# Cosine attention into a gated FFN on one core: 64-row products in five tiles, seven-product val one unit earlier, later loads of a batch, and a newly listed order

## The chip, the cores and the metric

The kernel runs on one core of a Trainium2 chip. The metric is device time in microseconds, the median over runs. A core has TensorE (PE; its weight loads are listed as PEld), VectorE (DVE), ScalarE (ACT), GpSimd (POOL) and SyncE (SP). Each engine runs its own list of instructions in order, and semaphores make one wait for another. DMAs are issued by SP, GpSimd and ScalarE. SBUF holds the data on 128 partitions; PSUM has eight banks of 128 x 512 fp32, into which TensorE writes.

## The reference

Eight batches, eight heads, 576 positions, 64 features a head. The attention is linear: the positive part of q and k is weighted by a cosine and a sine of the position, so that a head has 128 features, and

```python
r = np.maximum(x, 0.0)
phi(x) = np.concatenate([r * cos_w, r * sin_w], axis=-1)
kv = np.einsum('bhsf,bhsd->bhfd', phi(k), v)
z = np.sum(phi(k), axis=2)
num = np.einsum('bhsf,bhfd->bhsd', phi(q), kv)
den = np.einsum('bhsf,bhf->bhs', phi(q), z)[..., None] + 1e-06
attn = num / den
```

The result, as 4608 tokens of 512 features, goes through a gated feed-forward block with 1536 hidden features:

```python
g = x @ w_gate
val = x @ w_val
out = (g * sigmoid(g)) * val @ w_out
```

## The kernel before

**Tiles and groups.** A tile is 128 tokens: two slots of 64 positions of one batch, or the last slot of a batch and the first of the next (a two-batch tile: 4, 13, 22, 31). There are 36 tiles; four of them make a token group of 512 tokens, so there are nine groups, 0 to 8. For each batch the keys and values (`raw_kv`) become a key-value matrix per head, with z as a 65th column (`kv_job`, 72 products on quarters of the array). The queries become phi (`r_q`), which one DMA transpose turns (`phit`). For the first batches, tiles 4 to 8, TensorE turns the queries itself (`turned_tiles`), so that the cosine part and the sine part of a pair of heads lie in separate operands, which two accumulated products join. `tile_jobs` then computes a tile: products into two banks (L779 for tiles 4 to 8, L785 for the others), the denominator on ScalarE, its reciprocal and the multiplication on VectorE (`x`), and the turn of x (`turn_job`): by TensorE for tiles 4 to 7, by a DMA transpose on SP from tile 8 on. The DMA's turn is called a tile's turn below.

**The feed-forward block.** The 1536 hidden features are three units of 512 for gate and three for val. A plain product job is four products of 512 columns for 128 hidden features (`plain_fc`, `plain_val`, L904 and L1052), four of them a unit. The other form, `block_jobs`, computes a unit by the seven products of Strassen's scheme in Winograd's form, M1 to M7, each of four products with 256 columns (L977); sums of weights (`weight_sums`) and of x (`x_sum_jobs`) are made by VectorE. M1 is copied to a second bank (ScalarE), M7 is evacuated (`m7`), an addition puts M7 on M6 (VectorE), M5 is followed by a second addition, and M3 goes into the bank which that addition reads. `GATE_FROM` and `VAL_FROM` say from which group and unit on the seven products are used: gate from group 1, unit 0; val from group 2, unit 1. `silu_jobs` and `block_mul_jobs` form the hidden values `ht`; `token_sum_jobs` sums them; `out_jobs` makes the outputs with seven products P1 to P7 of the same kind (L1142). Group 0 is plain (`plain_out_jobs`, L1262).

**The order.** The first 27 us are a list written out by hand (`words`). All later work is a list of jobs. A planner (`order_once`) walks through modelled time with a cost for each job, due times, the banks and buffers that are free, and random shifts of the due times drawn by `SEEDS`, one seed for each `WINDOW` of modelled time; jobs are then issued in the order of their modelled starts. What it models decides only the order: on the chip, semaphores decide.

**Loads.** GpSimd issues the loads and most stores. The loads of a batch stand behind a hold, a tiny copy on GpSimd (`hold_job`) that reads what an earlier transfer wrote and so keeps the queue waiting for it. For batch 3 the hold reads the turn of tile 8; for the others it reads phi of the batch before, or for queries the turn of the last tile of a group.

Of the kernel before, what the change touches and what calls it, by code (L numbers as in the profile page):

```python
# [19 lines left out]
def kernel(  # L20
# [385 lines left out]

    xT = {}
# [175 lines left out]
    TAIL = {"PE": 206.0, "ACT": 160.0, "DVE": 140.0, "POOL": 150.0, "SP": 150.0}  # L583
    PAD = 12.0
# [19 lines left out]
    def sc(n, sbuf=False):  # L604
        return 69 + n / 1.2 + (27 if sbuf else 0) + PAD

# [29 lines left out]
    def relu_on(eng, out, in_):  # L636
# [11 lines left out]
    LOADED = {("k", 1): 440.0, ("v0", 1): 7580.0, ("v1", 1): 9080.0, ("sa", 1): 10080.0, ("sb", 1): 14480.0, ("q", 2): 22280.0,  # L648
              ("k", 2): 25580.0, ("v", 2): 29580.0, ("q", 3): 32380.0}
    WO_AT = ((0, 2, 11330.0), (2, 4, 12580.0), (4, 8, 16980.0), (8, 12, 19480.0))  # L650
    W_AT = {8: (1750.0, 3060.0), 10: (4820.0, 6130.0)}
# [19 lines left out]
    DEN_ON = {"ACT": 100}  # L671
# [35 lines left out]
    def kv_job(b, key, after):  # L707
# [12 lines left out]
        mm = pe(1404, fn, key, after=after, get=[r], chore=b > 1)  # L720
        outs = []
        for n in range(2):
            for i in range(2):
# [8 lines left out]
                outs.append(Job({"ACT": 402, "DVE": 450} if b == 1 else {"ACT": 402}, fn, after=[mm] + J_.get(("tiles", b - 2), []), put=[r]))  # L732
# [11 lines left out]
    def turn_job(t, x, after, by_pe=False, key=None):  # L744
        if not by_pe:
            def fn(j):
                nc.sync.dma_start_transpose(out=xT_of(t), in_=one(x_all, x))
            J_["xT", t] = Job({"SP": 1450}, fn, after=after + J_.get(("xT_read", t // OUT - 3), []), put=[x], tail=X_LAND, dma=(1430.0, X_SVC))
            return
        r = Room("bank")  # L750

        def fn(j):
            ps = bank(r).bitcast(FP16).rearrange("p (k x) -> p k x", x=P)
            for kc in range(KC):
                nc.tensor.transpose(out=ps[:, kc], in_=one(x_all, x)[:, kc * P:(kc + 1) * P], identity=ident16)
        mm = pe(230, fn, key, after=after, get=[r], put=[x])
# [5 lines left out]
    X_LAND = 4000.0  # L762
    X_SVC = 1030.0
    PHI_LAND = 11500.0

    def tile_jobs(t, key, by_pe=False):
# [3 lines left out]
        def fn(j):  # L770
            ps = bank(r)
            for e in range(2):
                for g in range(G):
                    for ms, b, c, n in parts_of(t):
                        if b < 2:
                            if g % 2:
                                continue
                            for w in range(2):
                                nc.tensor.matmul(  # L779
                                    out=ps[ms, e, g * D1:(g + 2) * D1],  # L780
                                    lhsT=late[:, 2 * (t % 2) + w, e, g // 2].rearrange("p c s -> p (c s)")[:, ms],
                                    rhs=(kvd1 if b else kvd)[:, e, g // 2, w].rearrange("p i x -> p (i x)"),
                                    start=w == 0, stop=w == 1)
# [5 lines left out]
        mm = pe(690 if 0 in bs else 455 if 1 in bs else 520 if len(bs) == 2 else 262, fn, key, after=sum((J_["kv", b] + turned_for(b, t) for b in bs), []), get=[r, one_at], chore=not by_pe)  # L789

        def view():
            return bank(r)[:, :, 0:2 * J * D1].rearrange("p e (y x) -> p e y x", x=D1)

        def fn(j):
            o, i_ = den_all[:, t % 4].rearrange("p (e y) o -> p e y o", e=2), view()[:, :, :, D:D1]
# [8 lines left out]
        rec = Job({"DVE": 132}, fn, after=[den])  # L804

        def fn(j):
            tt(out=one(x_all, x).rearrange("p (y e d) -> p e y d", e=2, d=D), in0=view()[:, :, :, 0:D],  # L807
               in1=rec_all[:, t % 4].rearrange("p (e y) o -> p e y o", e=2).to_broadcast([P, 2, 4, D]), op=ALU.mult)
# [8 lines left out]
    def load_job(b, nm, after, lands, behind):  # L817
        def fn(j):
            (load_turned if nm == "q" else load)(b, nm)
        J_["load", b, nm] = Job({"POOL": 1600 if nm == "q" else 780}, fn, after=after, tail=lands, behind=behind, dma=(1940.0, 2460.0) if nm == "q" else (470.0, 3770.0))  # L820

    def hold_job(read, after, put=()):
        def fn(j):
            nc.gpsimd.tensor_copy(out=hold2, in_=read())
        jb = Job({"POOL": 480}, fn, after=after, put=put)
# [854 lines left out]
```

## Time and profile before

| | |
|---|---|
| median of 3 runs | 298.38 us (298.32 to 298.6) |
| span of the profiled execution, first to last instruction | 296.4 us |
| TensorE busy | 291.1 us, 3244 products |
| VectorE busy | 252.0 us, 514 instructions |
| ScalarE busy | 199.4 us |
| GpSimd busy | 69.6 us |
| granted TensorE clock, mean | 0.998 |

The span is 2.0 us shorter than the median of the runs: what lies before its first and behind its last instruction isn't in it. Times in the profile's rows count from the span's start. A row of the chain gives the start, the duration and the group with its number of products; a row of the groups gives total busy time, mean ns of one, and the idle time ahead of it with what ended it. The end of a product is modelled: a group's shown end lies some 0.16 us behind the start of the next.

### The profile page before, as it was taken

To read this page: it belongs to the slowest core of one execution; us is meant where nothing else is said; L and a number is where in the kernel's file an instruction comes from. 1 tells how busy PE (TensorE), PEld (TensorE's weight loads), DVE (VectorE), ACT (ScalarE), POOL (GpSimd) and SP (SyncE) were. 2 spreads that over 40 slices of the span, in tenths; PEclk is the share of its full clock that TensorE was granted. 3 is DMA by queue.
4 is the path that set the end of the run, shared out by engine and by line. 5 is a ranking of instruction groups with operands and counts; after the bars stand their busy time and mean duration, and the time that the engine had idled before them with its cause. 6 is when DMAs were issued, how large, how long until landed. Compare 5 with 4: busy or idle time off the path is not lost.

```text
span 296.4 us, 8073 instructions
## 1 busy us (share of the span) xinstructions
PE 291.1 (98%) x3244; PEld 238.7 (81%) x3244; DVE 252.0 (85%) x514; ACT 199.4 (67%) x421; POOL 69.6 (23%) x122
## 2 busy tenths in 40 slices
PE   8999999999999999999999999999999999999994
PEld 4597465776787888898898889888988888888883
DVE  7878997879877999999988987998679868986883
ACT  6564346989559968985699589967465556565630
POOL 7963630003007012221352023200220050002000
PEclk9999999999999999999999999999999999999999
DMA  7999999997989997799996979940470046002026
GB/s 266 225 196 198 202 206 207 203 205 121 194 177 144 229 190 122 151 171 149 174 203 133 186 113 162 183 81 2 107 110 2 0 97 119 2 0 73 0 58 157
DMA packets 71973, 40.89 MB, mean 138 GB/s; under 512 B 48768, under 2 KB 68736, under 8 KB 71936
## 3 DMA queue, kind: packets, MB, share of 16 engines
q0 software_dynamic: 24800, 24.39, 49.1%
q1 hardware_dynamic: 46528, 15.47, 28.9%
q10 hardware_dynamic: 608, 0.52, 0.7%
q8 instruction: 25, 0.41, 0.6%
q14 instruction: 12, 0.10, 0.1%
HBM read 37.75 MB, written 9.44 MB: 159 GB/s over the span
## 4 chain that ended last, share of the span: by engine, by line
PE 97%; DVE 1%; issue 0%
PE banks L977 45%; PE banks L1142 24%; PE banks L1052 5%; PE banks L1262 4%; PE banks L438 4%; PE banks L904 4%; PE banks L187 3%; PE banks L716 3%; PE banks L785 2%; PE banks L779 1%; PE banks L372 1%; PE banks L1310 0%; PE banks L315 0%; PE banks L418 0%; PE banks L351 0%
## 5 line engine op out<-in xcount | busy, mean ns | idle before, releaser
L1111 POOL DMA_DIRECT2D out_dram<-ob x52 | 27.3, 532 | 104.8 <-ACT ob L630 69.7
L1036 ACT ACTIVATE sg<-banks 128x512 bf16<-128x512 f32 x72 | 41.3, 599 | 5.6 <-PE banks L977 5.4
L977 PEld LDWEIGHTS <-wg_sb 128*128 128x128 f16 x384 | 36.9, 98 | 6.3
L628 ACT COPY banks<-banks 128x512 f32<-128x512 f32 (+1 forms) x53 | 29.9, 572 | 17.5 <-PE banks L977 7.3
L1142 PEld LDWEIGHTS <-ht 128*128 128x128 f16 x384 | 37.4, 98 | 4.8
L1072 DVE TENSOR_TENSOR ht<-sg,banks 128x512 f16<-128x512 bf16 x60 | 39.9, 680 | 0.9 <-PE banks L977 0.6
L977 PEld LDWEIGHTS <-wgs_sb 128*128 128x128 f16 x368 | 35.7, 98 | 4.6
L997 DVE TENSOR_TENSOR banks<-m,banks 128x512 f32<-128x512 f32 x44 | 30.2, 693 | 10.6 <-ACT m L628 8.1
L977 PEld LDWEIGHTS <-wv_sb 128*128 128x128 f16 x320 | 31.0, 98 | 3.8
L977 PE MATMUL banks<-kvt,wgs_sb 128*128 128x256 f16 x236 | 33.4, 273 | 0.0
L1142 PEld LDWEIGHTS <-sums 128*128 128x128 f16 x288 | 27.9, 98 | 3.3
L630 ACT ACTIVATE ob<-banks 128x512 f32<-128x512 f32 x32 | 18.8, 596 | 15.9 <-PE banks L1142 15.2
L977 PE MATMUL banks<-xT,wg_sb 128*128 128x256 f16 x192 | 28.8, 273 | 0.0
L628 ACT COPY m<-banks 128x512 f32<-128x512 f32 x44 | 25.5, 590 | 4.4 <-PE banks L977 4.3
L1142 PE MATMUL banks<-wo_sb,ht 128*128 128x256 f16 x192 | 25.7, 273 | 0.0
L1142 PE MATMUL banks<-wt_sb,sums 128*128 128x256 f16 x192 | 24.9, 273 | 0.0
L977 PE MATMUL banks<-xT,wv_sb 128*128 128x256 f16 x160 | 24.0, 273 | 0.0
L1036 ACT ACTIVATE sg<-m 128x512 bf16<-128x512 f32 x24 | 15.1, 630 | 12.4 <-DVE m L1005 12.2
L807 DVE TENSOR_TENSOR x<-banks,rec 128x512 f16<-128x512 f32 x32 | 21.6, 686 | 1.5 <-DVE rec L803 0.2
L977 PE MATMUL banks<-kvt,wg_sb 128*128 128x256 f16 x168 | 22.4, 273 | 0.0
L1142 PE MATMUL banks<-wt_sb,ht 128*128 128x256 f16 x192 | 22.3, 273 | 0.0
L877 ACT ACTIVATE r_q<-raw_q,tanq 128x256 bf16<-128x256 bf16 x45 | 20.7, 510 | 0.1
(160 smaller groups left out, 544.7 us busy)
## 6 DMA issues: line engine op xcount, KB each, us to landing
out_dram<-ob POOLq DMA_DIRECT2D x52, 128.0 KB, 3.9
raw_kv<-in_k_dram POOLq DMA_DIRECT2D x7, 576.0 KB, 5.9
raw_q<-in_q_dram POOLq DMA_DIRECT2D x12, 288.0 KB, 10.7
raw_kv<-in_v_dram POOLq DMA_DIRECT2D x6, 576.0 KB, 8.3
out_dram<-ob SPq DMA_DIRECT2D x12, 128.0 KB, 2.5
wg_sb<-in_moe_w_gate_dram POOLq DMA_DIRECT2D x5, 256.0 KB, 8.9
wv_sb<-in_moe_w_val_dram POOLq DMA_DIRECT2D x5, 256.0 KB, 9.5
wo_sb<-in_v_dram SPq DMA_DIRECT2D x2, 576.0 KB, 4.2
```

What stands on the lines that cost most here:

```text
L438: nc.tensor.matmul(out=st["f", tg, fc, lo][i], lhsT=(wg_sb, wv_sb)[i][:, kc, fs], rhs=xT[tg][:, ts, kc], start=(kc == 0), stop=(kc == KC - 1))
L628: nc.scalar.copy(out=out, in_=in_)
L630: nc.scalar.mul(out=out, in_=in_, mul=mul)
L807: tt(out=one(x_all, x).rearrange("p (y e d) -> p e y d", e=2, d=D), in0=view()[:, :, :, 0:D], in1=rec_all[:, t % 4].rearrange("p (e y) o - ...
L877: nc.scalar.activation(out=home()[:, :, c, 1], in_=raws[b, "q"][:, :, c], func=AF.Relu, scale=tanq[:, c:c + 1])
L977: nc.tensor.matmul(out=to[:, i], lhsT=a[:, c, 2 * u + i], rhs=x()[:, :, c], start=first and i == 0 and c == 0, stop=c == KH - 1, skip_grou ...
L997: tt(out=bank(c), in0=one(m7_all, m).rearrange("p i x -> p (i x)"), in1=bank(b), op=ALU.add)
L1036: nc.scalar.activation(out=gates(rooms[w])[:, :, jh * HT:(jh + 1) * HT], in_=src, func=AF.Silu, scale=DOWN)
L1052: nc.tensor.matmul(out=bank(v), lhsT=wv_sb[:, kc, fc * P:(fc + 1) * P], rhs=xT[tg][:, :, kc], start=(kc == 0), stop=(kc == KC - 1))
L1072: tt(out=ht[:, 4 * u + w:4 * u + w + 3:2, jh * HT:(jh + 1) * HT], in0=gates(rooms[w])[:, :, jh * HT:(jh + 1) * HT], in1=src.rearrange("p ( ...
L1111: {"POOL": nc.gpsimd, "SP": nc.sync, "ACT": nc.scalar}[j.eng].dma_start(out=out_v[idx // NC, idx % NC][:, cols], in_=ob_of(t)[e * SH:(e + ...
L1142: nc.tensor.matmul(out=to, lhsT=a[:, kc, i * P:(i + 1) * P], rhs=b[:, kc], start=first and kc == 0 and i == 0, stop=kc == HC - 1, skip_gro ...
```

## The change

1. `VAL_FROM` becomes `(2, 0)`: val of group 2's unit 0 is made by seven products.
2. In tiles 4 to 8 a product over 128 rows (two heads of a pair, 130 columns) becomes two over 64 rows each (one head, 65 columns), which write to different banks; heads are therefore stored by row half, the turn by TensorE reads them back in order (`by_pairs`), and tile 8, which a DMA turns, multiplies in two halves.
3. Batch 3's loads are listed behind tile 11's turn instead of tile 8's.
4. The planner's costs, landing times, start times (`BUSY_AT`, `BANK_AT`), window (5 us instead of 10) and seeds are new, transfers end later or earlier in its model (`LATER`, `dma=`, `tail=`), and its random numbers come from a function of its own. So the order of all jobs behind the first 27 us is another.

```diff
-    TAIL = {"PE": 206.0, "ACT": 160.0, "DVE": 140.0, "POOL": 150.0, "SP": 150.0}
-    PAD = 12.0
+    TAIL = {"PE": 202.0, "ACT": 150.0, "DVE": 128.0, "POOL": 150.0, "SP": 150.0}
+    PAD = 1.0
...
-        mm = pe(1404, fn, key, after=after, get=[r], chore=b > 1)
+        mm = pe(1178, fn, key, after=after, get=[r], chore=b > 1)
...
-                nc.tensor.transpose(out=ps[:, kc], in_=one(x_all, x)[:, kc * P:(kc + 1) * P], identity=ident16)
+                nc.tensor.transpose(out=ps[:, kc], in_=one(x_all, x)[:, by_pairs(kc) * P:(by_pairs(kc) + 1) * P], identity=ident16)
...
                         if b < 2:
-                            if g % 2:
-                                continue
                             for w in range(2):
-                                nc.tensor.matmul(
-                                    out=ps[ms, e, g * D1:(g + 2) * D1],
-                                    lhsT=late[:, 2 * (t % 2) + w, e, g // 2].rearrange("p c s -> p (c s)")[:, ms],
-                                    rhs=(kvd1 if b else kvd)[:, e, g // 2, w].rearrange("p i x -> p (i x)"),
-                                    start=w == 0, stop=w == 1)
+                                for i in range(0 if g % 2 else 2):
+                                    rows = slice(i * D, (i + 1) * D)
+                                    nc.tensor.matmul(
+                                        out=ps[ms, i, (g + e) * D1:(g + e + 1) * D1],
+                                        lhsT=late[rows, 2 * (t % 2) + w, e, g // 2].rearrange("p c s -> p (c s)")[:, ms],
+                                        rhs=(kvd1 if b else kvd)[rows, e, g // 2, w, i], start=w == 0, stop=w == 1)
                             continue
...
-            tt(out=one(x_all, x).rearrange("p (y e d) -> p e y d", e=2, d=D), in0=view()[:, :, :, 0:D],
-               in1=rec_all[:, t % 4].rearrange("p (e y) o -> p e y o", e=2).to_broadcast([P, 2, 4, D]), op=ALU.mult)
+            x_, rec_ = one(x_all, x), heads(rec_all[:, t % 4])
+            if pairs and not by_pe:
+                for jj in range(J):
+                    ys = slice(2 * jj, 2 * jj + 2)
+                    tt(out=x_.rearrange("p (j i e d) -> p j i e d", i=2, e=2, d=D)[:, jj], in0=view()[:, :, ys, 0:D],
+                       in1=rec_[:, :, ys].to_broadcast([P, 2, 2, D]), op=ALU.mult)
+                return
...
-    VAL_FROM = (2, 1)
+    VAL_FROM = (2, 0)
...
-            if b == 3:
-                batch_loads(lambda: xT[2][0:1, 0, 0, 0:2], [J_["xT", 8]], names)
-            else:
+            if b > 3:
                 batch_loads(phit_read, J_["turned", b - 1], names)
         for t, s in tiles:
             tile_jobs(t, (tg, s / 4))
+            if t == 11:
+                batch_loads(lambda: xT[2][0:1, 3, 0, 0:2], [J_["xT", 11]], names)
...
-    BUSY_AT = {"PE": 0.0, "ACT": 0.0, "DVE": 750.0, "POOL": 0.0, "SP": 0.0}
+    BUSY_AT = {"PE": 1050.0, "ACT": 0.0, "DVE": 1600.0, "POOL": 0.0, "SP": 0.0}
...
-    LATER = 2400.0
+    LATER = 5000.0
...
-    WINDOW = 10000.0
+    WINDOW = 5000.0
```

71 lines of the change are left out of this document (41 added, 30 removed).

## The prediction

> **What bounds the kernel now.** I read the page first: its span, the busy time of each engine and the chain that ended last. Then I read TensorE's own waits.
>
> ```profile
> span 296.4 us, 8073 instructions
> PE 291.1 (98%) x3244; PEld 238.7 (81%) x3244; DVE 252.0 (85%) x514; ACT 199.4 (67%) x421; POOL 69.6 (23%) x122
> PE 97%; DVE 1%; issue 0%
> ```
>
> ```profile
> PE banks L187 <- DVE zeros L182: 1.0, 1, 1.0
> ```
>
> TensorE is busy 98% of the span and makes up 97% of the chain; its one listed wait is the first microsecond. So the span is the sum of TensorE's products, plus the few places where a product starts late. An edit helps only if it takes product time away or removes such a late start. It hurts if VectorE or a transfer gets behind TensorE. The runs' median is 298.38 us; the profiled execution's span is 296.4, and the 2.0 us outside it I take as unchanged, so differences of the span carry over to the median.
>
> The prices of products come from the chain in order of time (start, us, what):
>
> ```profile
> 41.47 1.17 PE banks L779 x24
> 43.21 0.97 PE banks L1262 x4
> 44.40 0.86 PE banks L1262 x4
> 45.26 0.47 PE banks L779 x8
> 62.09 1.18 PE banks L716 x63
> 65.98 0.26 PE banks L785 x8
> 70.22 1.73 PE banks L1052 x8
> 151.88 15.72 PE banks L977 x144
> 206.88 0.39 PE banks L785 x16
> ```
>
> A 512-column product takes 1.73/8 = 0.216 us, a 256-column one 15.72/144 = 0.109. Eight whole-array products of 65 columns take 0.26 (0.033 each), eight of 130 columns 0.47. The two-batch tile at 206.88 has sixteen products on half the array's columns: 0.39 (0.024 each). The 72 quarter-array products of a key-value job take 1.18 (0.016 each). A piece of four 512-column products takes 0.86 (44.40), but 0.97 right behind the split-array transposes (43.21): one run of split-array products costs about 0.10 extra.
>
> **The change, part by part.**
>
> *Val of group 2's first unit by blocks.* Sixteen 512-column products go (16 x 0.216 = 3.46) and 28 of 256 columns come (28 x 0.109 = 3.06): -0.40 on TensorE. It adds two ScalarE copies and, on VectorE, two additions and four smaller multiplications for four. With the spacing derived below (0.60 from PSUM, 0.34 from SBUF) VectorE goes from 4 x 0.60 = 2.40 to 5 x 0.60 + 0.34 = 3.34, or +0.9. That lies beside products as long as VectorE has room; see the third item.
>
> *Pairs of 64 rows in tiles 4 to 8.* Tile 4 has 16 products now and 32 afterwards; tiles 5 to 8 have 8 of 130 columns and get 16 of 65. Tile 4 now costs 1.17 - 0.47 = 0.70 with one 0.10 for the split, so 0.60 by itself. The changed products are in no row, so I bound them. For tiles 5 to 8: eight pairs at the whole-array price, 0.26; no overlap at all, 16 x 0.033 = 0.53; the nearest row is the sixteen half-array products, 0.39. I take 0.39: 4 x (0.47 - 0.39) = -0.32, ends -0.84 and +0.24. For tile 4: 32 quarter products at 0.016 give 0.52; half of it, as the columns are half, 0.26; I take the middle, 0.39: -0.21, ends -0.34 and -0.08. Runs of split-array work: in the changed order tiles 4 and 5 and the next transposes are one run (now 4 is one and the transposes are another), 6 and 7 are adjacent and form a new run, 8 is a new run: one more, +0.10, ends 0 and +0.30. Together -0.43.
>
> The Trainium skill, "TensorEngine Tiling (Array Packing)", section "Key Properties", says that a change of tiling mode drains TensorE. The 0.97 against 0.86 agrees; taken for every change of mode, 64x64 to 64x128 between tiles 4 and 5 included, two or three more drains would make the sum of this item about -0.2 instead of -0.43.
>
> Tile 8 gets its x product in two VectorE halves instead of one (about 0.1 more, beside products). Heads are stored in another order, which the tensor-engine transposes and the halves undo; no cost. One of the five ReLUs of turned tiles goes from ScalarE to VectorE, with the same cover.
>
> *The order.* All engines get new lists. Two late starts of the old one, which the list of waits does not show, stand in the timeline:
>
> ```profile
> 240.45 1.29 DVE L807 TENSOR_TENSOR x<-banks,rec 128x512 f16<-128x512 f32 x2 [0.24 <-DVE rec L803]
> 241.25 0.42 PE L785 MATMUL banks<-kv,phit 128*128 128x65 bf16 x8
> 241.79 0.61 PE L977 MATMUL banks<-kvt,vsums 128*128 128x256 f16 x4
> 287.71 0.43 DVE L1185 SCALAR_TENSOR_TENSOR banks<-r_q,banks 128x256 f32<-128x256 f32 x1 [0.35 <-ACT r_q L630]
> 287.76 0.49 PE L1142 MATMUL banks<-wt_sb,sums 128*128 128x256 f16 x3
> 288.19 2.78 PE L1142 MATMUL banks<-wt_sb,ht 128*128 128x256 f16 x24
> ```
>
> Tile 35's products (0.26 of work) were followed after 0.54: TensorE waited 0.28 for the x product, whose bank it takes 0.05 after VectorE's end at 241.74. Near the end three products (0.33) were followed after 0.43: 0.10. In the changed order the next products stand further from these VectorE results (the last group's addition has 0.43 us of room where it had none), so 0.38 goes.
>
> The rows also give the delays. Two VectorE operations in 1.29, the last showing 0.69 (L997 below), are spaced 0.60, some 0.08 less than is shown; so L1072 from SBUF is spaced 0.34 and L803 0.12. The eight products show 0.42 for 0.26 of work: a result leaves 0.16 after the next group may start, and its reader starts some 0.04 later. So a way from product through VectorE to product is 0.20 + 0.68 + 0.05 = 0.93.
>
> ```profile
> L997 DVE TENSOR_TENSOR banks<-m,banks 128x512 f32<-128x512 f32 x44 | 30.2, 693 | 10.6 <-ACT m L628 8.1 <-PE banks L977 1.8 <-ACT sg L1036 0.3
> L1013 DVE TENSOR_TENSOR sg<-m,banks 128x512 f16<-128x512 f32 x20 | 13.6, 681 | 1.6 <-PE banks L977 1.6
> L1072 DVE TENSOR_TENSOR ht<-sg 128x512 f16<-128x512 bf16 x20 | 8.3, 416 | 0.0
> L803 DVE RECIPROCAL rec<-den 128x8 f32<-128x8 f32 x32 | 6.1, 197 | 5.4 <-ACT den L797 5.2
> 97.00:110.00 13.00, 13.00 (x119) 11.40 (x118) 12.11 (x23) 10.49 (x21) 2.01 (x4) 1.00 1.15 214
> 152.00:168.00 16.00, 16.00 (x149) 14.32 (x148) 14.40 (x27) 14.54 (x31) 3.77 (x7) 1.00 0.93 168
> ```
>
> (The last two rows are stretches: length, then busy time of TensorE, weight loads, VectorE, ScalarE, GpSimd.) I lay out the changed list by adding the prices above from 27.1 us on; a "place" is a time in that sum. The shortest distance is at the end of group 2. Val's product M5 of unit 2 ends at 105.51; between it and M3, which needs the addition that follows M5, stand only M4 and tile 16 (0.44 + 0.26), so M3's place is 106.21. VectorE has begun a 0.60 sum at 105.24, adds from 105.84 to 106.52, and M3 starts at 106.57: 0.36 late. The half product of P1 behind it needs the multiplication after that addition (to 107.12): another 0.17. New waits: +0.53; ends 0, if VectorE is half a microsecond ahead there, and the price of the slower rival below.
>
> *Batch 3's loads.* SP now issues the turns of tiles 8, 9, 11 and 10 before them, and GpSimd's hold waits for tile 11's turn; behind it on GpSimd stand the three loads, then four stores, then the hold for batch 3's phi and batch 4's loads. Landing times in the loads' stretch (first the turns of all groups, then 68 to 90 us):
>
> ```profile
> DMA to landing us min/median/max: 2.4/4.8/12.2
> raw_kv<-in_k_dram POOLq DMA_DIRECT2D x2, 576.0 KB, 5.9
> raw_kv<-in_v_dram POOLq DMA_DIRECT2D x2, 576.0 KB, 8.9
> raw_q<-in_q_dram POOLq DMA_DIRECT2D x2, 288.0 KB, 11.9
> phit<-r_q SPq DMA_TRANSPOSE x1, 14.6
> DVE kvt L950 <- DMA xT<-x: 1.4, 1, 1.4
> ```
>
> Now two turns lie among these loads and come late (the 12.2), and VectorE waits 1.4 for them, without cost to TensorE. Afterwards the turns are issued at places 72.6 to 75.3 with nothing beside them, at 2.4 each. The loads go out near 77 to 81, so they land at about 83, 88 and 93; their readers stand at 89.0 (keys), 92.4 (values) and 95.3 (queries). I cost the move at nothing: the cover is 2 to 6 us. If it were gone, each microsecond would hold VectorE or ScalarE and soon TensorE. Batch 3's phi still shares its time with the loads; issued at 76.7 and 14.6 long it lands at 91, and what waits for it are batch 4's loads, read at 105. Of the later turns the shortest ways from issue to reader are 4.5 us (tile 14, place 104.7) to 5.4 (tile 27), about the median landing of 4.8; there nothing else is in flight, so they cost nothing.
>
> **The sum.** -0.40 - 0.43 - 0.38 + 0.53 = -0.68 us: a span of 295.7, and 297.7 us by the runs.
>
> **The rivals.**
>
> *The pairs run at the full rate and no new wait appears.* -0.40, then -0.84 - 0.34 + 0.10 for the pairs, and -0.38: -1.86, about 296.5; with one of the two, near 296.9. For it: TensorE hardly waits now. Against: the half-array row is 0.39, not 0.26.
>
> *The new waits eat it.* If the waits are 1.1 instead of 0.53, the time is 298.3, no change. For it: the saving is small and the changed order's other distances are as short as the old ones (about as many under 0.2 us).
>
> *The pairs do not overlap.* 0.53 per tile instead of 0.39, tile 4 at 0.52, and two more splits: the item becomes about +0.4, the time 298.5. The Trainium skill, "TensorE: Matmul & The Clock Gate", section "LDWEIGHTS (loading the stationary operand)", says that a weight load's time goes by its columns and not by its rows, so twice the loads would take twice the time if loads were the limit. By that rule it is this rival; its tiling page says instead that tiles load and multiply in parallel. No row here has 64-row products over all columns.
>
> *VectorE becomes the bound: slower.* In the changed list the operations in places 97 to 110 are 16 at 0.60, 8 at 0.34, 4 reciprocals at 0.12 and one ReLU of about 0.4: 13.2 us in 13.0, against 12.1 busy in the old order; in 152 to 168 it is 15.8 in 16.0, against 14.4. In the old order VectorE stood idle 0.9 and 1.6 in these stretches, for operands from TensorE and ScalarE. If it does so again, TensorE waits 0.2 + 0.9 = 1.1 in the first and 1.6 - 0.2 = 1.4 in the second, 2.5 in all instead of 0.53: 299.7. It decides from 1.2 us of such idle time in both together (0.68 saved plus the 0.53 counted); halfway the time is 298.9. Against it: each wait of TensorE lets VectorE catch up.
>
> **How the numbers follow.** The forecast has 0.38, the greater gain 0.11; these are the faster cases, 0.49. Waits that eat it 0.17, and pairs that do not overlap 0.08: within 0.2%, 0.25. VectorE as the bound 0.26: slower. I call 0.2% (0.6 us) the least that a measurement of this kernel can tell from no change. The likeliest case alone reaches from 297.2 to 298.0. The range goes from 296.7, near the greater gain, to 299.3, most of the way to VectorE's price.
>
> **What would show it.** After: TensorE's 512-column val group has 16 products fewer and the 256-column ones 28 more; tile 5's sixteen products take 0.35 to 0.42; tiles 6 and 7 stand together with one longer piece behind them; no late start near 233 to 242; M3 of group 2's last val unit 0.2 to 0.5 late at about 107 us; VectorE over 95% busy from 98 to 111 and from 153 to 169; the turns of tiles 8 to 11 at 2.4 to 3 us. The prediction is wrong if TensorE's waits add up to over 1.2 us, if tile 5 takes 0.5, or if a load's reader starts at its landing with TensorE idle behind it.

## The result and the profile after

The changed kernel takes 309.7 us (308.55 to 310.51, 4 runs) against 298.35 us (298.04 to 298.6, 4 runs) of the kernel before: a ratio of 1.0377, 95% interval 1.0346 to 1.0408. It is 3.8% slower; the forecast was 297.7 us in a range of 296.7 to 299.3. The profiled execution took 310.47 us, with a span of 308.7, 12.3 longer than before.

The top of the page after: span, busy time, the granted clock in forty slices, and the chain by engine.

```profile
span 308.7 us, 8181 instructions
PE 294.3 (95%) x3304; PEld 240.6 (78%) x3304; DVE 252.3 (82%) x518; ACT 199.6 (65%) x422; POOL 68.6 (22%) x122
PEclk9999999999999989999999998999999999999999
PE 49%; DMA 28%; issue 13%; ACT 4%; POOL 3%; DVE 1%; ACTq 0%; DVEq 0%; POOLq 0%
```

VectorE's and ScalarE's busy times are within 0.3 us of those before (252.0 and 199.4); what changed is the chain. TensorE made up 97% of it and now 49%, and 28% are transfers. TensorE's own waits say the same (who waited for whom: us in total, times, longest):

```profile
PE banks L990 <- DMA xT<-x: 5.1, 2, 3.7
PE banks L718 <- DVE x L820: 1.6, 1, 1.6
...
PE banks L757 <- DVE x L820: 0.4, 1, 0.4
...
PE banks L784 <- ACT phit L630: 0.2, 1, 0.2
```

The stretches show where (length, then busy time of TensorE, weight loads, VectorE, ScalarE, GpSimd; then granted clock, DMA share, GB/s). First the kernel before, then the changed one:

```profile
90.00:120.00 30.00, 30.00 (x351) 25.53 (x340) 26.73 (x52) 26.05 (x58) 8.13 (x15) 1.00 1.05 179
160.00:200.00 40.00, 40.00 (x451) 35.70 (x449) 36.11 (x68) 33.06 (x74) 6.07 (x12) 1.00 0.85 144
```

```profile
90.00:120.00 30.00, 26.74 (x321) 22.47 (x319) 24.86 (x50) 22.55 (x48) 7.24 (x13) 0.94 1.09 183
160.00:200.00 40.00, 35.11 (x403) 30.16 (x401) 30.36 (x60) 28.00 (x64) 9.39 (x18) 0.96 1.07 144
200.00:290.00 90.00, 90.00 (x937) 80.41 (x936) 74.15 (x140) 54.14 (x107) 10.44 (x21) 1.00 0.33 61
```

TensorE is idle 3.3 us in the first stretch and 4.9 in the second, at a reduced mean clock; from 200 us on nothing is lost. Both stretches hold a phi whose transposes took far longer than 14.6 us, the longest one before. The transfers of the changed kernel issued from 78 to 97 us (kind, count, KB each, median us from issue to landing):

```profile
raw_kv<-in_k_dram POOLq DMA_DIRECT2D x1, 576.0 KB, 10.0
raw_kv<-in_v_dram POOLq DMA_DIRECT2D x1, 576.0 KB, 13.8
raw_q<-in_q_dram POOLq DMA_DIRECT2D x2, 288.0 KB, 15.6
phit<-r_q SPq DMA_TRANSPOSE x1, 20.4
```

And those issued from 160 to 180:

```profile
raw_q<-in_q_dram POOLq DMA_DIRECT2D x2, 288.0 KB, 16.6
xT<-x SPq DMA_TRANSPOSE x4, 8.0
phit<-r_q SPq DMA_TRANSPOSE x1, 20.0
```

How a late transfer reaches TensorE is seen in the timeline of the changed kernel (start, us, engine, what; in brackets the idle time ahead and who ended it; three stretches of it):

```profile
98.89 0.46 DVE L282 TENSOR_SCALAR r_q<-raw_q 128x1152 bf16<-128x1152 bf16 x1 [1.81 <-DMA phit<-r_q]
99.27 0.68 DVE L820 TENSOR_TENSOR x<-banks,rec 128x512 f16<-128x512 f32 x1
...
100.01 1.25 PE L718 MATMUL banks<-v,raw_kv 64*64 64x130 bf16 x72 [1.65 <-DVE x L820]
...
112.91 1.03 PE L990 MATMUL banks<-xT,wg_sb 128*128 128x256 f16 x4 [1.36 <-DMA xT<-x]
113.74 1.06 PE L990 MATMUL banks<-xT,wv_sb 128*128 128x256 f16 x4
...
183.26 0.51 ACT L880 ACTIVATE r_q<-raw_q,tanq 128x256 bf16<-128x256 bf16 x1 [5.63 <-DMA raw_q<-in_q_dram]
...
183.72 0.60 PE L990 MATMUL banks<-xT,wg_sb 128*128 128x256 f16 x4 [3.75 <-DMA xT<-x]
```

- **Near 98 to 116.** Phi 3 lands at 98.8. VectorE has come to a ReLU of batch 4's queries, which needs phi 3 landed (it writes `r_q`, from which phi 3 is turned), and waits 1.81; tile 12's x, which has nothing to do with phi 3, stands behind that ReLU, and TensorE waits for it. Batch 4's loads, held on phi 3, go out at 99.4 instead of 88.8 and now share their time with the turns of tiles 12 to 15. The turn that TensorE waits for at 112.91 had been issued at 105.6 and took 7.2 us.
- **Near 160 to 194.** Batch 7's query load goes out at 165.4, behind the start of phi 6 (163.2). It takes 17.8 us, ScalarE waits 5.63 for it, and the turns in the same stretch take 8.0 in the median.
- **The clock.** The products at 112.91 and 113.74 last 0.83 and 0.85 for four (start to start) instead of 0.437. The granted clock is half of full speed from 112.94 to 116.35 and from 184.62 to 188.03 (rows of the first of the two stretches stand in the last section); each costs about 1.6 us. The shortest run of the changed kernel, 308.55 us, had a mean clock of 1.000, so the clock is the smaller part of the loss.

I summed, for every job of TensorE, the distance to the next job's start less its price from the prediction's rows (0.35 for a tile of pairs). Before, 1.9 us are left over; after, 15.7. Of the 15.7, 11.5 stand at the places of late transfers (1.8 at 97.8; 3.2 from 110.9 to 116.3; 3.9 at 179.6; 1.6 from 184.6 to 188; 1.0 at 193.7; the half clock's 3.2 us are among them), 2.7 at other late starts, and the rest is small distances, as before. The prices themselves add up to 1.1 us less, and the first job starts 0.4 us earlier: 13.8 - 1.1 - 0.4 = 12.3, the whole difference.

### The profile page after: what moved, and what is told of

It reads as the page before. It is cut to its first block, busy times and chain, and to the rows that moved or that the text cites. A ratio compares the mean times of both kernels' runs of the same rounds, so it can differ in the third digit from the quotient of the medians.

```text
span 308.7 us, 8181 instructions
## 1 busy us (share of the span) xinstructions
PE 294.3 (95%) x3304; PEld 240.6 (78%) x3304; DVE 252.3 (82%) x518; ACT 199.6 (65%) x422; POOL 68.6 (22%) x122
## 4 chain that ended last, share of the span: by engine, by line
PE 49%; DMA 28%; issue 13%; ACT 4%; POOL 3%; DVE 1%; ACTq 0%; DVEq 0%; POOLq 0%
PE banks L990 30%; PE banks L1155 16%; DMA raw_q<-in_q_dram 9%; DMA phit<-r_q 7%; DMA wg_sb<-in_moe_w_gate_dram 6%; DMA raw_kv<-in_v_dram 3%; DMA xT<-x 2%; PE banks L789 1%; PE banks L718 1%; DMA wo_sb<-in_v_dram 1%; ACT r_q L890 1%; POOL wv_sb L269 1%; POOL wg_sb L268 1%; ACT raw_kv L280 1%; POOL out_dram L1124 1%
## 5 line engine op out<-in xcount | busy, mean ns | idle before, releaser
L1085 DVE TENSOR_TENSOR ht<-sg,banks 128x512 f16<-128x512 bf16 x63 | 42.3, 681 | 3.6 <-PE banks L990 3.2
L630 ACT COPY banks<-banks 128x512 f32<-128x512 f32 (+1 forms) x54 | 30.5, 573 | 22.0 <-PE banks L990 11.3
L1010 DVE TENSOR_TENSOR banks<-m,banks 128x512 f32<-128x512 f32 x45 | 31.0, 693 | 13.2 <-ACT m L630 5.4
L990 PEld LDWEIGHTS <-wgs_sb 128*128 128x128 f16 x372 | 36.4, 99 | 5.5 <-issue 0.5
L990 PEld LDWEIGHTS <-wv_sb 128*128 128x128 f16 x336 | 32.5, 98 | 4.4
L990 PE MATMUL banks<-kvt,wgs_sb 128*128 128x256 f16 x240 | 34.5, 275 | 0.3 <-DVE x L820 0.3
L990 PE MATMUL banks<-xT,wg_sb 128*128 128x256 f16 x192 | 29.5, 278 | 5.1 <-DMA xT<-x 5.1
L630 ACT COPY m<-banks 128x512 f32<-128x512 f32 x45 | 26.4, 591 | 4.1 <-PE banks L990 3.8
L990 PE MATMUL banks<-xT,wv_sb 128*128 128x256 f16 x168 | 25.3, 276 | 0.0
L1155 PE MATMUL banks<-wt_sb,ht 128*128 128x256 f16 x192 | 23.8, 282 | 0.0
L1049 ACT ACTIVATE sg<-m 128x512 bf16<-128x512 f32 x24 | 15.1, 628 | 12.2 <-DVE m L1018 12.0
L292 DVE TENSOR_TENSOR v<-raw_kv,tab 128x1152 bf16<-128x1152 bf16 x27 | 19.3, 753 | 2.1 <-DMA raw_kv<-in_v_dram 2.1
```

The source lines that it names most:

```text
L292: nc.vector.tensor_tensor(out=v2s[b == 1][:, g, :, :, 0:D], in0=(first if b == 0 and g == 0 else {"v": raw_of(b, "v")})["v"][:, g].unsquee ...
L630: nc.scalar.copy(out=out, in_=in_)
L990: nc.tensor.matmul(out=to[:, i], lhsT=a[:, c, 2 * u + i], rhs=x()[:, :, c], start=first and i == 0 and c == 0, stop=c == KH - 1, skip_grou ...
L1010: tt(out=bank(c), in0=one(m7_all, m).rearrange("p i x -> p (i x)"), in1=bank(b), op=ALU.add)
L1049: nc.scalar.activation(out=gates(rooms[w])[:, :, jh * HT:(jh + 1) * HT], in_=src, func=AF.Silu, scale=DOWN)
L1085: tt(out=ht[:, 4 * u + w:4 * u + w + 3:2, jh * HT:(jh + 1) * HT], in0=gates(rooms[w])[:, :, jh * HT:(jh + 1) * HT], in1=src.rearrange("p ( ...
```

## The experiments

Two theories at first. **T:** transfers that are in flight together delay each other, and the changed order puts phi 3 and phi 6 into the same time as loads. **D:** the new order fills VectorE's list so far that everything behind it is late, and long transfers are a by-catch. The medians of the kernel before beside these runs were 298.7 to 298.8 us. In all runs that move a job, the list of the planner stands and only the named jobs are put elsewhere in it (`listed` is the list by modelled starts, `move(jobs, at)` puts jobs behind another one); a load's hold then reads what the load is put behind.

### The pairs alone

Item 2 of the change (pairs in tiles 4 to 8) in the kernel before, order unchanged:

```diff
-                                nc.tensor.matmul(out=ps[ms, e, g * D1:(g + 2) * D1], lhsT=late[:, ...][:, ms], rhs=kvd[:, ...])
+                                for i in range(0 if g % 2 else 2):
+                                    rows = slice(i * D, (i + 1) * D)
+                                    nc.tensor.matmul(out=ps[ms, i, ...], lhsT=late[rows, ...][:, ms], rhs=kvd[rows, ..., i])
```

> The kernel before with the 64-row pairs of tiles 4 to 8 alone; the listed order is the old one. The prediction's price of the pairs: -0.43 us, 297.9. If the pairs do not overlap: +0.4, 298.8. If they run at the whole-array rate, as tile 6 of the changed kernel suggests (0.25 us from its first product to the next job): -0.6 to -1.0, 297.4 to 297.8.

Measured: 299.84 us (297.82 to 300.87 in eleven runs, 304.62 in one), ratio 1.0021, interval 0.9994 to 1.0048: no difference that can be told, with a wide spread. The profiled execution was the shortest run, with a span of 295.9 against 296.4 of the kernel before. In its chain (start, us, what) the prices of the tiles can be read:

```profile
41.55 0.74 PE banks L785 x48
44.97 0.35 PE banks L785 x16
45.65 0.35 PE banks L785 x16
46.00 1.83 PE banks L1276 x8
54.35 0.35 PE banks L785 x16
54.70 1.85 PE banks L991 x16
```

Tiles 4 and 5 take 0.74 together instead of 1.17, tiles 6, 7 and 8 take 0.35 each instead of 0.47. Eight 512-column products behind tile 7 take 1.83 instead of 1.73, sixteen of 256 columns behind tile 8 1.85 instead of 1.75: about 0.10 for each return to the whole array. The 0.35 of tile 8 holds another 0.10 ahead of its first product: the four products before it last 0.53 from their first start to its first, instead of 0.437. So a tile that stands by itself gains almost nothing (0.35 and 0.10 for 0.47), and the gain is that of tiles 4 and 5, 0.43. The pairs do overlap: from the first to the last start, tile 8's sixteen products take 0.23. Whether 0.5 us of product time reaches the end was not seen by the medians.

### The two moves of loads in the changed kernel

Batch 3's hold and loads go behind phi 2's landing; batch 7's query load goes behind tile 16's turn; and both.

```diff
-                batch_loads(lambda: xT[2][0:1, 3, 0, 0:2], [J_["xT", 11]], names)
+                batch_loads(lambda: phit[2][0:1, 0, 0, 0], [J_["xT", 11]], names)
...
+    move(l3, J_["turned", 2][0])
+    move(l7, J_["xT", 16])
```

> The changed kernel with batch 3's hold and its three loads moved on GpSimd's queue alone: behind phi of batch 2 (it landed at 63.0) instead of behind tile 11's turn. Theory T (the loss is transfers that share their time: batch 3's phi, issued 0.4 us ahead of the three loads, took 20.4 us, and what follows it came late): phi of batch 3 takes 7 to 9 us, batch 4's loads go out near 87 instead of 99, TensorE's waits between 97 and 116 (1.8 at 97.8, about 4 from 109.7 on) go, and the time falls by 5 to 6 us to about 304. Theory D (VectorE has no room in these stretches): the waits stay, 309 to 310.

> The changed kernel with batch 7's query load moved alone: behind tile 16's turn (landed at 125.2) instead of behind tile 23's. Theory T: phi of batch 6 (20.0 us beside this load, 163 to 183) takes 7 to 10 us, ScalarE does not wait 5.6 us for the queries, TensorE's 3.9 at 179.6 and the 1.6 behind it go: 5 to 6 us less, about 304. Theory D: no change, 309 to 310. Batch 5's loads come some 1.5 us later in either case, with 5.5 us of room.

> Both moves together. Theory T: the two parts add up, 297.5 to 299.5, so near the kernel before; what is left is the 1.0 us at 193.7 and the short waits near 41 to 45. Theory D: 308 to 310.

Measured: batch 3's loads alone 306.02 us (ratio 1.0231, 1.0189 to 1.0273), batch 7's query load alone 304.18 (1.0176, 1.0127 to 1.0225), both 301.9 (1.0092, 1.0059 to 1.0125). So 7.8 us of the 11.4 lost come back by moving four loads on GpSimd's queue, with every other engine's list the same. T's 304 came out for the query load; for batch 3's loads it was missed by 2 us, and for both together (297.5 to 299.5) by 2.4. In the run with both moves, the transposes of phi 3 have the time to themselves (transfers issued from 78 to 97 us):

```profile
phit<-r_q SPq DMA_TRANSPOSE x1, 7.3
```

The two stretches are nearly full again in that run:

```profile
90.00:120.00 30.00, 29.74 (x366) 26.01 (x364) 29.23 (x58) 24.12 (x53) 7.66 (x14) 1.00 0.86 151
160.00:200.00 40.00, 39.81 (x453) 35.49 (x453) 36.50 (x69) 33.35 (x76) 8.03 (x15) 1.00 0.91 160
```

7.3 us for the same phi that took 20.4; with only the second move, phi 6 took 10.4 instead of 20.0. VectorE is busy 29.23 us in the first stretch, against 24.86 in the changed kernel and 26.73 before, and TensorE loses 0.26 there: D falls. One wait of TensorE is new in that run, 1.6 us for a turn. It opened behind 138.4, since batch 7's query load now goes out at 122 and, with batch 5's loads and eight stores, lies beside the turns of tiles 17 to 19, which took 10.1 us in the median.

### The move by itself, in the old order

The kernel before with batch 3's loads behind tile 11's turn, nothing else:

```diff
-                batch_loads(lambda: xT[2][0:1, 0, 0, 0:2], [J_["xT", 8]], names)
+                batch_loads(lambda: xT[2][0:1, 3, 0, 0:2], [J_["xT", 8]], names)
...
+    move(l3, J_["xT", 11])
```

> The kernel before, with one part of the change alone: batch 3's two key and value loads and batch 4's query load are held until tile 11's turn has landed, in the old order of everything else; nothing is left out. T (transposes that share their time with loads issued right behind them take much longer): tile 11's turn now lands near 74 to 75 instead of 83.9, the loads go out near 75, right behind the transposes of batch 3's phi (issued 73.2), and phi 3 takes 18 to 21 us instead of 14.6, landing at 92 to 94; its first reader stood 0.1 us behind it, so TensorE comes to wait some 2 to 5 us between 93 and 110. Time 302 us (300.5 to 304.5). Rival N (only the new order's list makes the transfer late, the move by itself is harmless): phi 3 lands by 89 and the time stays within 1 us of the kernel before.

Measured: 306.44 us (306.22 to 306.97), ratio 1.0264, 1.0248 to 1.028. The move alone costs 7.7 us, more than expected, but not by the way that was expected. The transfers that this kernel issues from 73 to 79 us:

```profile
raw_kv<-in_k_dram POOLq DMA_DIRECT2D x1, 576.0 KB, 10.5
raw_kv<-in_v_dram POOLq DMA_DIRECT2D x1, 576.0 KB, 12.6
phit<-r_q SPq DMA_TRANSPOSE x1, 11.2
```

ScalarE in its timeline:

```profile
85.85 1.25 ACT L281 ACTIVATE raw_kv<-raw_kv 128x576 bf16<-128x576 bf16 x2 [6.07 <-DMA raw_kv<-in_k_dram]
```

Phi 3 was shorter than before (11.2), and the turns took 2.4. The loads themselves were late: the keys landed at 85.8, where ScalarE's ReLU had stood since 79.8; that ReLU held an output copy, VectorE waited for its bank, and TensorE 5.3 us for VectorE. So the price is the same in kind, the victim another: here the keys, in the changed kernel phi 3.

### The move undone in the changed kernel

Batch 3's loads behind tile 8's turn again, the rest of the new list as it stands:

```diff
-                batch_loads(lambda: xT[2][0:1, 3, 0, 0:2], [J_["xT", 11]], names)
+                batch_loads(lambda: xT[2][0:1, 0, 0, 0:2], [J_["xT", 11]], names)
...
+    move(l3, J_["xT", 8])
```

> The changed kernel with that one part undone in its list: batch 3's key and value loads and batch 4's query load are held on tile 8's turn again, as before the change, and go out near 70 instead of 79; the rest of the list stands. Nothing is left out. T (whatever shares its time with these four transfers is late): phi 3, issued near 78.4, lands at 90 to 94 instead of 98.8 and the 1.8 us wait at 97.8 with its slow products up to 116 goes (3.5 to 4 us), but the turns of tiles 9 to 11, issued 74 to 78, now stand behind the loads and land near 83 to 86 where TensorE reads the first at 80.5: 2 to 3 us come back there. Time 308.2 us (306.8 to 309.3). Rival U (the place behind tile 8's turn is free of cost in the new list too): 306.0 us, as with the loads behind phi 2.

Measured: 311.24 us (310.1 to 312.23), ratio 1.0416, 1.0391 to 1.0441. Undoing this part does not give its loss back: the kernel is no faster than the changed one. The transfers issued from 74 to 80 us:

```profile
xT<-x SPq DMA_TRANSPOSE x3, 8.1
phit<-r_q SPq DMA_TRANSPOSE x1, 9.6
```

Phi 3 is down to 9.6 and landed at 89.0 (T had 90 to 94), but the turns of tiles 9 to 11 now took 7.3 to 9.3; TensorE waited 3.9 us for one, up to 84.3, and had the half clock from 85.0 to 88.4. The estimate of 2 to 3 us for these turns was too low.

### Earlier loads in the old order, with the pairs

The kernel of the first experiment, and batch 3's loads on phi 2's landing:

```diff
-                batch_loads(lambda: xT[2][0:1, 0, 0, 0:2], [J_["xT", 8]], names)
+                batch_loads(lambda: phit[2][0:1, 0, 0, 0], [J_["xT", 8]], names)
...
+    move(l3, J_["turned", 2][0])
```

> The kernel before in its own order, with the pairs of the change in tiles 4 to 8 and with batch 3's loads held on phi 2's landing (out near 63 to 66 instead of 69 to 72); nothing else of the change. Nothing is left out. T: the loads are through by 78, so turns 10 and 11 (8.8 and 12.2 us beside them) and phi 3 (14.6 us, read 0.1 us after it lands) land 4 to 6 us sooner, nothing of it waits when TensorE arrives 0.5 us earlier, and the pairs' own 0.5 us shows: 297.6 us (297.1 to 298.3), 0.4 to 0.5% faster than before. Rival W (the pairs' gain is given back at other transfers that are just in time, phi 4 and batch 5's loads with 0.4 to 1.1 us to spare): 299 us or above, as with the pairs alone.

Measured: 308.23 us (305.75 to 309.38 in five runs, 311.92 in one), ratio 1.029, 1.0259 to 1.0321. A plain miss: this was meant as a version that beats both kernels. The transfers issued from 66 to 74 us:

```profile
xT<-x SPq DMA_TRANSPOSE x3, 10.2
```

TensorE's waits:

```profile
PE banks L1066 <- DVE x L821: 4.0, 1, 4.0
PE banks L991 <- DMA xT<-x: 2.6, 2, 1.5
```

Phi 3, issued at 79.0 when the loads were all but through, took 7.3. But three of the turns of tiles 8 to 11, issued at 65.7 to 70.7 right behind the loads, took 10 to 12 us instead of 2.4, and in this order TensorE and VectorE read the first of them at 72: 4.0 us of waiting, then 1.1 for the next one, with half the clock from 75.1 to 85.3. I had looked at what lay behind the new place, not at what lay beside it.

### How much of phi 3 is issued ahead of the loads

The changed kernel with batch 3's loads held on tile 10's turn, so that they go out 1.7 us behind the start of phi 3's issue instead of 0.4:

```diff
-                batch_loads(lambda: xT[2][0:1, 3, 0, 0:2], [J_["xT", 11]], names)
+                batch_loads(lambda: xT[2][0:1, 2, 0, 0:2], [J_["xT", 11]], names)
...
+    move(l3, J_["turned", 3][0])
```

> The changed kernel with batch 3's loads held on tile 10's turn, the last of the four, instead of tile 11's: they go out near 80.4 instead of 78.8, so 2 us behind the start of phi 3's issue (78.4) instead of 0.4 us. Nothing is left out. T1 (what counts is how much of phi 3 is issued ahead of the loads: it took 11.2 us with a lead of 1.6 us in the old order, 20.4 with 0.4 us in the changed one): phi 3 lands at 89 to 92, the 1.8 us wait at 97.8 goes and with it the lateness of batch 4's loads and of turns 12 to 15; about 306.3 us (305.3 to 307.5), as with the loads behind phi 2. T2 (any load that is in flight in phi 3's time holds it up, whichever was issued first): phi 3 lands at 97 or later, and the time stays at 309 to 311.5.

Measured: 307.52 us (306.49 to 308.16), ratio 1.0283, 1.0252 to 1.0315, at the upper end of T1. Of the transfers issued from 78 to 97 us:

```profile
phit<-r_q SPq DMA_TRANSPOSE x1, 11.5
```

A lead of 1.7 us instead of 0.4, and phi 3 took 11.5 instead of 20.4; the wait at 97.8 is gone. The packets show why a lead of 1.4 us more is worth 9. First phi 3 alone, from 81 to 85 us in the run with both moves; then the changed kernel from 87 to 92, where q0 carries the loads and q1 the transposes (queue, kind, packets, MB, share of 16 engines):

```profile
q1 hardware_dynamic: 3394, 0.87, 114.6%
```

```profile
q0 software_dynamic: 715, 0.79, 99.9%
q1 hardware_dynamic: 713, 0.18, 29.5%
```

Alone, the transposes send 849 packets a microsecond. Beside the loads they send 143, one for one with packets of the loads, which are four times as large (1.1 KB and 0.25 KB). In both kernels the loads' first packets move some 5 us behind their issue, at 83.8 in the changed kernel and at 85.7 here. From the start of phi 3's issue up to then, 3097 of the transpose queue's 5066 packets had gone in the changed kernel, and 4846 here. The 1969 that were left in the changed kernel take 13.8 us at 143 a microsecond, up to 97.6; phi 3 landed at 98.8. So T1 was right, and what counts is how many of phi 3's packets are out before the loads' first. For phi 6 the counts don't show this: from 170 to 180 in the changed kernel there were 1771 packets of transposes and 603 of loads and stores, and how the query load slowed it stays open.

TensorE has a new wait, 2.2 us that end at 125.6: VectorE had stood 3.3 us for phi 4, which took 14.2 beside batch 5's query load. And near 177 to 186 the loss around phi 6 stands as in the changed kernel.

### Other places for batch 7's query load, and TensorE's own order

Three more runs start from the one with both moves. The first puts batch 7's query load behind batch 6's value load instead of tile 16's turn; the second adds five swaps of neighbours in TensorE's list (numbers of jobs: one that is ready is listed ahead of one that waited); the third holds the load on phi 6.

```diff
-    move(l7, J_["xT", 16])
+    move(l7, J_["load", 6, "v"])
...
+    ahead(84, 72)
+    ahead(45, 76)
+    ahead(214, 202)
+    ahead(539, 446)
+    ahead(554, 446)
...
-    move(l7, J_["load", 6, "v"])
+    move(l7, J_["turned", 6][0])
```

> The changed kernel with batch 3's loads behind phi 2's landing, as in the run with both moves, and batch 7's query load behind batch 6's value load (held on phi 5's landing, out near 151) instead of behind tile 16's turn (out near 122). Nothing is left out. T: the turns of tiles 17 to 19, which took 9 to 10 us beside that load, land 4 to 6 us sooner, and the 1.8 us wait at 138.4 goes: 300.1 us (299.5 to 300.7) where the run with both moves had 301.9. Rival S (the load is as much in the way wherever it stands): turns 21 and 23 and phi 6 land 4 to 6 us later instead, a wait of about the same size opens between 170 and 180, and the time stays at 301.4 or above.

> The kernel of the last run with five TensorE jobs listed ahead of neighbours that wait: the transposes of tiles 6 and 7's features ahead of tile 4, an output product ahead of tile 4's turn, a value product ahead of the gate product that waits at 58.6, and two ready products of the next unit ahead of the one that waits at 109.5. Nothing is left out. T (what is left after the transfers are the order's own late starts: 0.47 at tile 4, 0.57 before its turn, 0.14 at 58, 0.58 at 108.8 to 109.5): 1.2 to 1.7 us less than the last run, 298.6 us (297.9 to 299.2), level with the kernel before or just under it. Rival V (VectorE's pace makes these waits, so they come back a little later in the same stretch): less than 0.5 us goes, 299.7 or above.

> The run with five TensorE jobs listed ahead, with batch 7's query load held on phi 6's landing (out near 171, ahead of batch 7's key and value loads) instead of behind batch 6's value load (out near 148). Nothing is left out. T: turn 21, which took 11 us beside that load, lands 4 to 6 us sooner and the 1.7 us wait near 160 goes; the load lands near 176, ScalarE stands up to 1.5 us for it at 175. Its profiled run 299.8 us or less, median 300.0 us (298.5 to 301.5). Rival S (the stretch from 125 to 180 has no free place for the load): a wait of 1.5 us or more opens between 170 and 195, and the median stays at 301.5 or above.

Measured: 302.08 us (299.86 to 304.21), ratio 1.011, 1.0072 to 1.0148; with the swaps 304.23 (300.84 to 305.18), 1.0163, 1.012 to 1.0206; with the load behind phi 6 300.67 (300.43 to 301.14), 1.0065, 1.0051 to 1.0079. In the first, turns 17 to 19 took 5.2 instead of 10.1 and the wait at 138 was gone; but turn 21, issued at 150.8 behind the load, took 11.3 (transfers issued from 146 to 153 us):

```profile
raw_q<-in_q_dram POOLq DMA_DIRECT2D x2, 288.0 KB, 9.9
xT<-x SPq DMA_TRANSPOSE x1, 11.3
```

Its longest wait of TensorE, 2.4 us that end at 162.9, is for the x behind that turn. So S, the rival, had the mechanism, though the wait came ahead of 170. The same kernel took 299.9 and 304.2 in two other runs; what makes that spread isn't shown, as one run has a profile. Behind phi 6 the turn takes 6.1 and the runs lie within 0.7 us. This is the fastest version found of the changed kernel, still 0.65% slower than the kernel before. Its waits of TensorE:

```profile
PE banks L990 <- DVE kvt L963: 1.0, 2, 0.8
PE banks L1155 <- DVE sums L1106: 0.7, 1, 0.7
```

The times expected, 300.1, 298.6 and 300.0, were missed by 2.0, 5.6 and 0.7 us, the last within its range. The swaps can't be judged by the two medians, whose ranges overlap. In the profiles the late starts near 41 to 46 lost part of their size, and the 0.58 at 109 to 111 did not go: it became one wait of 0.7 for VectorE (the second row). There rival V was right: VectorE sets the pace at that place.

### The changed kernel without its pairs

The first of these three with tiles 4 to 8 as before the change:

```diff
-                                for i in range(0 if g % 2 else 2):
-                                    rows = slice(i * D, (i + 1) * D)
...
+                            if g % 2:
+                                continue
```

> The kernel with both loads moved (batch 7's query load behind batch 6's value load), the list unchanged, but tiles 4 to 8 computed as before: one product over the whole array for a pair of heads, their x in the old layout. Nothing is left out. T (a tile of pairs takes 0.35 for 0.47, but tile 4 stands 0.47 us on a copy of the state either way): 0 to 0.6 us above the kernel with the pairs, 300.4 us (299.9 to 300.9). Rival P (the pairs hold up VectorE or ScalarE behind them and are a part of the loss): 0.5 us or more below the kernel with the pairs.

Measured: 304.96 us (304.48 to 305.22), ratio 1.0211, 1.0194 to 1.0227: 2.9 us above the kernel with the pairs, where 0 to 0.6 was expected. The pairs are no part of the loss. How much of the 2.9 is theirs stays open: the first job of the profiled execution starts 0.8 us later too, and other transfers meet.

## Why the prediction was wrong

**The failed step** is the fourth part, the sentence "I cost the move at nothing: the cover is 2 to 6 us", with the two that follow it: phi 3 "issued at 76.7 and 14.6 long", and of the later turns "nothing else is in flight, so they cost nothing". All durations there were taken from the kernel before, as if a transfer had a length of its own. Phi 3 was issued at 78.4 and took 20.4; the loads went out at 78.8 to 80.9, about as predicted, but took 10.0, 13.8 and 15 to 16 instead of 5.9, 8.9 and 11.9 and landed at 88.8, 93.3 and 97.1 instead of 83, 88 and 93. Near 160 to 184 the new order put batch 7's query load beside phi 6, which I had not looked at. The runs show it: with the loads moved away at both places, 7.8 of the 11.4 us are back.

What I should have added up is the work of a stretch, and how it is shared: while loads are in flight, a transpose gets one packet for each of theirs, a sixth of its pace alone. The four load transfers of batch 3 and batch 4's queries, with the transposes beside them, last some 18 to 20 us wherever they stand: 69.3 to 87.8 before, 78.4 to 98.8 after, 73.8 to 91.6 with the move in the old order, 63.3 to 81.5 in the run with earlier loads. The order only decides which of them lands last, and the cost is what the lists hang on that one. The old list fits the first of these; of the other places, each with a phi, a turn or a key load as the last, none tried was free in both lists.

**The other terms, by their steps.**

- *Val by blocks, -0.40.* The counts are as predicted, 16 products of 512 columns fewer and 28 of 256 more (the rows of 512 columns before and after). No run has this part alone, so its price isn't measured by itself:

```profile
L1052 PE MATMUL banks<-xT,wv_sb 128*128 128x512 f16 x64 | 16.1, 379 | 0.0
L1065 PE MATMUL banks<-xT,wv_sb 128*128 128x512 f16 x48 | 12.0, 379 | 0.0
```

- *Pairs, -0.43.* Mis-sized, on the good side: about -0.7. Tiles 4 and 5 take 0.43 less than before, tiles 6 and 7, which are adjacent in the changed order, some 0.25 less, and tile 8 next to nothing. The sixteen products of a tile take about 0.25, the rate of the greater gain, and not the 0.39 of the nearest row; that row has in it a 0.10 of the kind that follows, and I had seen one only at the end of a run. The starts of the products show some 0.10 at every change of form: 0.31 instead of 0.22 for the 512-column product ahead of tile 8 (at 64.7 in the changed kernel), and 0.12 both between tiles 4 and 5 (at 41.6) and at the return behind tile 8 (65.2), where neighbours within a tile start 0.003 to 0.036 apart. So the reading of the Trainium skill, "TensorEngine Tiling (Array Packing)", section "Key Properties", with a drain for every change agrees with the trace; the sum of -0.2 that was worked out with it did not come, since the tiles themselves were cheaper.
- *The order, -0.38.* The two old late starts are gone (nothing is lost from 200 to 290).
- *The order, +0.53.* Measured 0.42 and 0.16 at 109.7 to 110.9, for 0.36 and 0.17. Not foreseen were 0.47 within tile 4, whose later products wait for ScalarE's copy of the state, and 0.57 ahead of its turn. I had laid out the list with tile 4 at its price, without asking when all its operands are there. As an estimate, without the late transfers the changed kernel would have a span of 308.7 - 11.5 = 297.2, 0.8 (0.3%) above the kernel before: slightly slower, not faster.
- *VectorE as the bound, 299.7.* The sign of this rival came out, its cause did not. VectorE was busy 12.0 of the 13 us from 98 to 111, and 13.40 of 14 from 97 to 111 in the fastest version, whose only large late start there is 0.8 us, at 111.5, where the rival had 1.1. In the other stretch, 152 to 168, that version's TensorE is busy for all of it.
- *The pairs don't overlap.* Refuted by the 0.35: the two products of a pair start 0.003 to 0.010 us apart, so twice the weight loads on half the rows went beside each other.
- None of the rivals was about transfers, although the profile had the warning: a turn of 12.2 us beside one of 2.4, the same operation.

## What to carry to other kernels

A transfer's duration in a profile is that of the company it had; before moving a load, add up all that will be in flight with it, with its packets as well as its bytes, and ask which landing comes last and what stands behind it in the lists. A wait of one in-order engine for something it needs much later (a ReLU of the next batch's queries) stops everything listed behind it. And a wait of TensorE can cost more than its length: the half clock behind it can come on top.

## What the runs showed of the hardware

- **Transposes beside loads.** The same DMA transpose of a phi took 7.3 us alone, 11.2 and 11.5 with loads issued 1.5 and 1.7 us behind its start, and 20.4 with loads 0.4 us behind. A turn took 2.4 alone and up to 12.2. The DMA engines were full throughout (a share of 0.97 from 78 to 100 us). The Trainium skill, "DMA: Bandwidth & Descriptors", section "Queues, rings and completion order", says that each DMA engine goes round its queues packet by packet. The trace agrees: 715 packets of the loads and 713 of the transposes from 87 to 92 us. Equal turns by packet are what makes the lead count: with packets of 0.25 KB beside packets of 1.1 KB, the transposes got less than a fifth of the bytes there (0.18 of 0.97 MB). This is shown for phi 3, not for phi 6. Why the loads' first packets come 5.0 to 5.7 us behind their issue when a phi was issued just ahead, and 1.5 us in the kernel before (69.3 to 70.7), stays open.
- **The clock after a wait.** The granted clock is either full or half in these profiles, and between 25 and 280 us it changes only at steps of 3.41 us that run through the whole execution. Four of these steps in the changed kernel (length, then TensorE's busy time; the granted clock is the third number from the end):

```profile
95.88:99.29 3.41, 2.48 (x23) 2.07 (x22) 1.60 (x5) 2.53 (x6) 0.40 (x1) 1.00 0.60 187
99.29:102.70 3.41, 2.69 (x86) 2.45 (x86) 3.41 (x7) 2.66 (x8) 3.36 (x6) 1.00 0.51 56
```

```profile
109.53:112.94 3.41, 1.79 (x20) 1.07 (x19) 3.41 (x8) 2.47 (x6) 0.00 (x0) 1.00 1.51 126
112.94:116.35 3.41, 3.41 (x17) 2.35 (x18) 3.04 (x9) 1.17 (x2) 1.48 (x3) 0.50 1.28 281
```

The wait of 1.65 us that ends at 100.0 lies across a border, with 0.9 and 0.7 us idle on its two sides, and the clock stays full. The shorter wait of 1.36 that ends at 112.9 lies in one step, with a late start of 0.26 ahead of it: 1.6 us idle, and the next step has half the clock. The wait of 3.75 that ends at 183.7 leaves 2.5 us idle in the step up to 184.6, and the half clock begins there, 0.9 us behind the wait. Over all 14 profiles, in that part of the execution, every step at the full clock with 2.0 us or more of idle time was followed by one at half, none with 1.5 or less was, and of the four between 1.6 and 1.7 one was. The Trainium skill, "TensorE: Matmul & The Clock Gate", section "What's actually happening", gives a free-running window of about 3.4 us and a half clock after an idle one. The length and the free running agree; that a window idle for half its length can be enough is what these runs add.
- **Spread.** The kernel with batch 7's query load ahead of turn 21 took 299.9 to 304.2 us from run to run; with the load behind phi 6 it was 300.4 to 301.1.
